# The last group of an FFT convolution in halves, its output sums split into 96 rows first and 32 rows side by side after

## The chip, the cores and the metric

The kernel runs on one core of a Trainium2 chip. The metric is the device time of one execution in microseconds (us), as the median of several runs. TensorE (PE) multiplies matrices into PSUM, VectorE (DVE) and ScalarE (ACT) compute and copy PSUM results into SBUF, GpSimd (POOL) computes tables, SyncE (SP) issues nearly all DMA transfers, and ACT issues a few. A DMA queue issues in order: a transfer that waits for a semaphore holds up all transfers behind it on the same issuing engine.

## The reference

Two state-space convolutions (A and B) run over the same input `u` (2048 steps, 512 channels), and a gate mixes them:

```python
K = jnp.einsum("dn,dnl,dn->dl", Cc, P, dB).real          # a filter for each channel, 2048 long
Yf = Uf * Kf                                             # FFTs over 4096 points
y = irfft2(Yf)[..., :L] + u * Dskip
g = _sigmoid((x * gate_w).sum(-1, keepdims=True))
return g * a + (1 - g) * b
```

All is float32. The output is 2048 x 512 numbers.

## The kernel before, in words

The 512 channels are worked on in eight chunks `c` of 64; a chunk has 128 columns (64 channels of A and of B). For each chunk sixteen-channel steps build the filter from sine and exponential tables (`tables`: ACT, POOL and DVE), and TensorE makes it (`kgen`, L595) and transforms it to a first stage (`first`, L612) in a buffer `xa` or `xb`. That fills nearly all of the run.

Then comes the convolution of a chunk. `conv(c, j)` for j = 0 to 7 makes an eighth of the spectrum with four matmuls (`spectrum`, L625; eight instructions in the trace, since a float32 matmul is recorded as two) and multiplies it on DVE with the spectrum of `u` (L701) into a buffer `y`, of which there are three. After every second `j`, `back(c, U)` (U = 0 to 3, a "unit") transforms back: 32 matmuls (`inv`, L721), each of 64 rows by 64 columns, four of which lie side by side in the array, write two PSUM banks; two copies of 128x512 numbers bring them to `z`; two transfers of 256 KB write `z` to a scratch array `zb` in DRAM; and gathers read `zb` back so that each unit fills 32 partitions of a buffer: for the last chunk `xa`, as one 512 KB transfer for units 0, 1 and 2, and as four transfers of 128 KB, one for each output block, for unit 3. All transfers are issued through `dma` (L295), the copies through `copy` (L300 on ACT, L302 on DVE).

With all four units there, `fin(c, k)` for the output blocks k = 0 to 3 sums over all 128 partitions with the weights `gsi` (the gate is in them): 16 matmuls of 128 rows by 64 columns (L757), one copy of 128x256, and one 128 KB transfer to the output. `stay_awake` (L770) puts six matmuls of 128x512 on TensorE between the sums of chunk 6, and uses their result for nothing.

Nothing is planned at run time: `ORDER` is a list, written out by hand, of all operations by number (a `b` behind a number takes the second engine allowed). Each engine works through its own operations in that order. Buffers are rings: `z` has two, `y` three, the PSUM ring `c` four banks, `s` and `sq` one tile of two banks each. In the end of the list before, TensorE's order is: the inverse of unit 0; spectra 5 and 4; inverse of unit 1; spectra 7 and 6; inverse of unit 2; sums of chunk 6, block 0; inverse of unit 3; sums of blocks 1 and 3 of chunk 6; the six matmuls of `stay_awake`; block 2 of chunk 6; blocks 3, 2, 1 and 0 of chunk 7. SP's order there is: writes of unit 1; gather of unit 0; writes of unit 2; gather of unit 1; writes of unit 3; gather of unit 2; the four gathers of unit 3 with one output transfer among them; the last output transfers.

Of the kernel before, what the change touches and what calls it, by code (L numbers as in the profile page):

```python
# [21 lines left out]
F1, F2 = 32, 64  # L22
# [90 lines left out]
795 796 772 797 1526 1527 1538 798 773 799 1539 785 1553 786b 800 801 787 1554 1540 1541b 1550 1549 1542b 1551 802 803b 886  # L113
# [4 lines left out]
873 1904b 863 864 852 874 875 876 853b 1585 1586 1587 888 892 889 865 893 877 894 895 906 296 896 866 925 878 867 926 897 879  # L118
# [3 lines left out]
1597 1546 1577 1590 1908 1592 1560 1576 1575 1593 1591 331 1612 1915 947 937 948 334 1905 313 314 315b 1916b 316 1917 1578  # L122
1598 1599 323 324b 326 327b 325 960 961 1613 317 949 1614 962 963 318b 1912 320 1918 1020 969 970 988 971 972 987 1023 989 950
951 1913b 964 965 1919b 973 1909 1609 1914 321 322 319 974 975 328 1627 976 920 922 921 977 1910b 978 979 966 967b 990 968 993
# [83 lines left out]
def ssm_mix(ctx: ExitStack, tc: tile.TileContext, a, out, dry=False):  # L208
    slots, pools, shapes = {}, {}, {}

    def ring(tag, n, shape, dtype=F32, space=None):
        slots[tag] = n
        shapes[tag] = shape, dtype
        pools[tag] = space

    ring("xa", 1, [128, F1, CH])
    ring("xb", 1, [128, F1, CH])
    ring("uin", 2, [128, 8, L2])
    ring("par", 2, [128, 5, CH], I32)
# [590 lines left out]
    for c in range(NCH):  # L810
        for k in range(4):
            fin(c, k)
# [45 lines left out]
```

## Time and profile before

| | us |
|---|---|
| median of 3 runs | 432.73 |
| lowest, highest | 431.26, 434.06 |
| the profiled execution, its own time | 429.2 |
| its span (first to last instruction) | 427.4 |
| mean granted TensorE clock in it | 0.994 |

Over the whole span the engines are busy: PE 90%, DVE 90%, ACT 85%, POOL 84%. POOL has done its last work before the last tenth of the span, and the last slices of the profile are of another kind than the rest: there DVE, ACT and POOL are mostly idle, while PE and the DMA engines are not. In the chain of waits, "DMA zb<-z" is a write of `z` to the scratch array, "xa<-zb" a gather for the last chunk, "c<-xa,gsi" the sums of the last chunk and "c<-f,gsi" those of chunks before. Some pieces of the chain are put down to a neighbour: a semaphore is known only by the transfer that the profile links to it.

### The profile page before, as it was taken

How to read it: one execution, taken by the hardware profiler on the slowest of the kernel's cores; microseconds unless marked ns; L12 is line 12 of the kernel's file. 1: busy time of each engine (PE TensorE's matmuls, PEld its weight loads, DVE VectorE, ACT ScalarE, POOL GpSimd, SP SyncE). 2: the span in 40 equal slices, each digit the busy share in tenths (PEclk: the TensorE clock that was granted, in tenths of full speed). 3: DMA queues.
4: the chain of work that ended last, by engine and by line, in shares of the span. 5: the costliest groups of instructions: out<-in, count | busy, mean ns of one | idle time of the engine just before them, and what ended most of it. 6: DMA issues, size and time to landing. Idle time of an engine off the chain costs nothing.

```text
span 427.4 us, 21919 instructions
## 1 busy us (share of the span) xinstructions
PE 384.0 (90%) x9636; PEld 342.3 (80%) x9636; DVE 385.1 (90%) x547; ACT 361.3 (85%) x522; POOL 358.7 (84%) x291
## 2 busy tenths in 40 slices
PE   5898887899998989998989999999889979999994
PEld 5787776788877878888979988888778969898964
DVE  5799999999999999998989999999999999996620
ACT  2889999899998999998889989999899898992211
POOL 1896989899999999997999999999999999970000
PEclk9999999899999999999999999999999999999999
DMA  7968845178882677687385555574777576667794
GB/s 240 287 214 269 263 149 180 28 221 224 257 247 79 197 215 203 201 240 230 109 221 177 176 170 156 166 220 145 225 209 217 143 220 199 172 205 216 219 274 137
DMA packets 79855, 84.63 MB, mean 198 GB/s; under 512 B 7600, under 2 KB 62768, under 8 KB 79664
## 3 DMA queue, kind: packets, MB, share of 16 engines
q1 hardware_dynamic: 79472, 82.96, 65.9%
q8 instruction: 76, 1.25, 1.3%
q10 hardware_dynamic: 288, 0.26, 0.2%
q14 instruction: 19, 0.16, 0.1%
HBM read 51.55 MB, written 31.65 MB: 195 GB/s over the span
## 4 chain that ended last, share of the span: by engine, by line
PE 32%; ACT 23%; DVE 15%; POOL 11%; issue 10%; DMA 7%; SPq 1%; ACTq 0%; DVEq 0%; POOLq 0%
PE c L625 8%; PE c L612 8%; PE c L721 6%; PE c L595 5%; POOL ang L277 4%; DVE mr L287 4%; ACT s L290 4%; POOL mr L277 4%; ACT sq L290 4%; ACT ang L290 3%; PE c L757 3%; DVE ei L277 3%; ACT z L300 2%; DMA zb<-z 2%; DVE y L701 2%
## 5 line engine op out<-in xcount | busy, mean ns | idle before, releaser
L287 DVE SCALAR_TENSOR_TENSOR mr<-sq,mr 128x1024 f32<-128x1024 f32 (+1 forms) x128 | 117.5, 946 | 3.1 <-ACT sq L290 3.0
L277 POOL TENSOR_TENSOR mr<-ml 128x1024 f32<-128x1024 f32 x52 | 101.6, 1955 | 2.5 <-PE c L595 2.0
L277 DVE TENSOR_TENSOR ei<-s,mr 128x1024 f32<-128x1024 f32 x64 | 77.6, 1213 | 2.6 <-POOL mr L277 1.0
L595 PE MATMUL c<-mr 128*32 128x64 f32 x2048 | 64.5, 223 | 8.0 <-DVE mr L287 3.0
L290 ACT ACTIVATE s<-ang 128x1024 f32<-128x1024 int32 x64 | 66.2, 1035 | 6.0 <-DVE ei L287 3.4
L277 POOL TENSOR_TENSOR ang<-sa 128x512 int32<-128x512 int32 x64 | 69.8, 1092 | 0.3
L277 POOL TENSOR_TENSOR ang<-par,cint 128x512 int32<-128x512 int32 x64 | 67.2, 1052 | 3.1 <-ACT sq L290 3.1
L701 DVE TENSOR_TENSOR y<-c,u 128x1024 f32<-128x1024 f32 x57 | 68.7, 1214 | 1.1 <-PE c L625 0.8
L290 ACT ACTIVATE ang<-ang 128x1024 f32<-128x1024 int32 x64 | 67.9, 1061 | 0.9
L290 ACT ACTIVATE sq<-ang 128x1024 f32<-128x1024 f32 x64 | 66.1, 1033 | 2.9 <-DVE mr L287 1.5
L277 POOL TENSOR_TENSOR mr<-mh 128x512 f32<-128x512 f32 x64 | 68.3, 1071 | 0.0
L595 PE MATMUL c<-ei 128*32 128x64 f32 x2048 | 63.6, 221 | 1.4 <-issue 1.4
L612 PE MATMUL c<-small,kt 128*64 128x128 f32 x1024 | 63.0, 275 | 1.6 <-ACT z L300 0.9
L595 PEld LDWEIGHTS c<-mr 128*32 128x32 f32 x2048 | 48.4, 110 | 19.0 <-issue 10.0
L721 PE MATMUL c<-y,vv 64*64 64x128 f32 x1792 | 57.9, 273 | 3.9 <-issue 2.6
L612 PEld LDWEIGHTS c<-small,kt 128*64 128x64 f32 x1024 | 55.5, 137 | 5.4 <-ACT z L300 1.3
L625 PE MATMUL c<-xa,w 128*128 128x128 f32 x384 | 53.0, 284 | 4.6 <-ACT z L300 2.3
L721 PEld LDWEIGHTS c<-y,vv 64*64 64x64 f32 x1792 | 50.1, 133 | 8.4 <-issue 3.7
L625 PE MATMUL c<-xb,w 128*128 128x128 f32 x384 | 51.9, 283 | 5.3 <-DVE c L420 1.6
L625 PEld LDWEIGHTS c<-xb,w 128*128 128x128 f32 x384 | 45.7, 191 | 10.7 <-issue 2.4
L625 PEld LDWEIGHTS c<-xa,w 128*128 128x128 f32 x384 | 45.9, 191 | 9.4 <-ACT z L300 2.9
L595 PEld LDWEIGHTS c<-ei 128*32 128x32 f32 x2048 | 50.4, 111 | 1.6 <-issue 1.5
(108 smaller groups left out, 594.5 us busy)
## 6 DMA issues: line engine op xcount, KB each, us to landing
zb<-z SPq DMA_DIRECT2D x64, 256.0 KB, 3.6
u<-us SPq DMA_DIRECT2D x57, 256.0 KB, 4.1
f<-zb SPq DMA_DIRECT2D x112, 128.0 KB, 3.9
us<-z SPq DMA_DIRECT2D x32, 256.0 KB, 3.1
uin<-in_uk_dram SPq DMA_DIRECT2D x16, 256.0 KB, 4.1
f<-in_ut_dram SPq DMA_DIRECT2D x8, 512.0 KB, 5.6
out_dram<-o SPq DMA_DIRECT2D x28, 128.0 KB, 3.2
par<-prd SPq DMA_DIRECT2D x7, 320.0 KB, 4.2
```

The costliest lines, as they stand in the source:

```text
L277: lambda e: (dve if e == "dve" else pool).tensor_tensor(out=out(), in0=in0(), in1=in1(), op=o),
L287: lambda _: dve.scalar_tensor_tensor(out=out(), in0=in0(), scalar=s, in1=in1(), op0=o0, op1=o1), reads, writes, port=port)
L290: op("act", "act", n, lambda _: act.activation(out=out(), in_=in_(), func=func, **{k: v() if callable(v) else v for k, v in kw.items()}), ...
L300: act.activation(out=o(), in_=i(), func=AF.Copy)
L595: pe.matmul(ps[32 * j:32 * j + 32, o], x[:, 4 * o + j, 64:96], x[:, 4 * o + j, 0:64], start=part == 0, stop=part == 1, tile_position=(0, 3 ...
L612: pe.matmul(t(*ps[g // 4])[64 * r:64 * r + 64, 128 * (g % 4):128 * (g % 4) + 128], t(*x)[:, g], t("small")[:, 128 * r:128 * r + 128], star ...
L625: pe.matmul(view()[:, :, k], t("w2", j // 2)[:, 4 * (j % 2) + k], t(*x1)[:, 4 * j + k], start=True, stop=True)
L701: op("dve", "tt1", 1024, lambda _: dve.tensor_tensor(out=t(*y).rearrange("p h s f d -> p h s (f d)"), in0=fv().rearrange("p s f d -> p s ( ...
L721: pe.matmul(bank_of(x)[64 * e:64 * e + 64, CH * q:CH * q + CH], v[:, 0:64] if h else v[:, 32:96], t(*ys[f // 4])[64 * x:64 * x + 64, h, :, ...
L757: pe.matmul(t(*ps)[64 * r:64 * r + 64, DC * i:DC * i + DC], t("gsi")[:, 4 * k + i, s, 64 * r:64 * r + 64], t(*f)[:, 8 * k + 2 * i + r, DC ...
```

## The change

It touches the last chunk, its order, and two small buffers.

- **The gathers of units 0, 1 and 2 of the last chunk** stay one 512 KB transfer each, but `xa` is now laid out as four eighth-pieces of 8x128 numbers with one spare number behind each (`eighths`), so that a row of 16 KB no longer lies in one piece. `cube` gives the old view of `xa` to all others.
- **Unit 3 of the last chunk in halves** (`w` = 0, 1). A half of the inverse (16 matmuls) needs only one of the two products `y`. It writes halves of two banks of the ring `c`; each half has two copies of 128x256 and two writes of 128 KB.
- **Unit 3's rows over four groups of 32 partitions.** Its four gathers put block k's rows on partitions 32k to 32k+31 of a buffer of the ring `ei` (`spread`), all at the same columns. Four further transfers of 128 KB (`g3`) copy unit 3's weights, rows 96 to 127 of `gsi`, likewise into a buffer of the ring `mr`.
- **The last sums in two steps** (`last_fins`). First, for each block, two matmuls with zero weights clear 256 columns of a PSUM bank, and 16 matmuls sum over the 96 rows of units 0 to 2 (`first_units`). Then the 32 rows of unit 3 are added, two blocks at a time: 32 matmuls of 32 rows by 64 columns whose row groups differ by block (`last_unit`). Blocks 2 and 3 come first. `stay_awake` is gone.
- **The order.** All that lies before the last 250 or so operations stays (it is only renumbered). At the end, TensorE has: inverse of unit 0; spectrum 4; inverse of unit 1; spectra 5 and 7; inverse of unit 2; spectrum 6; sums of chunk 6, block 3; first half of unit 3; block 0; second half; blocks 2 and 1; the first sums of blocks 0, 1, 2, 3; the last sums of 2 and 3; the last sums of 0 and 1. DVE makes products 2, 4, 5, 6, 7 in this order, then copies one piece of the first half. ACT copies the other piece of the first half and both of the second. SP has: writes of unit 1; gather of unit 0; writes of unit 2; gather of unit 1; gather of unit 2; the first half's two writes; an output transfer, `g3` of block 2, another output transfer, `g3` of block 3; the gathers of unit 3 for blocks 2 and 3; output transfers. ACT's queue has the second half's two writes, the gathers of unit 3 for blocks 0 and 1, and output transfers. `g3` of blocks 0 and 1 stand on SP much earlier, among the gathers of chunk 6.
- **`dummy`**, one column used to load a table of ACT at the start, becomes a fifth column of `gate_w`. The gathers of chunks 0 to 6 get an access pattern written with one dimension less; what they move is the same.

The core of the diff (the order's numbers left out):

```diff
-    ring("xa", 1, [128, F1, CH])
+    ring("xa", 1, [128, 4 * (8 * CH + 1)])
...
         last = c == NCH - 1
         ys = [("y", c, 2 * U + i) for i in range(2)]
-        ps = [(("s", "sq")[U % 2], "inv", U)] if last else [("c", "inv", c, U, x) for x in range(2)]
+        wide = last and U < 3
+        parts = 2 if last and not wide else 1
...
+        for w in range(parts):
+            ps = [(("s", "sq")[U % 2], "inv", U)] if wide else [("c", "inv", c, U, x, w) if last else ("c", "inv", c, U, x) for x in range(2)]
+            qs = slice(4 // parts * w, 4 // parts * (w + 1))
...
+            op("pe", "inv", 128 // parts, inv, [*(ys if parts == 1 else ys[w:w + 1]), ("vv", U // 2)], ps, table="square")
+            for x in range(2):
+                copy(512 // parts, lambda x=x, qs=qs: t(*z)[:, x, qs].rearrange("p q k -> p (q k)"),
...
+                if parts > 1:
+                    g = 8 * U + 4 * x
+                    dma(128, lambda g=g, x=x, qs=qs: t(*zb)[g + qs.start:g + qs.stop].rearrange("g p k -> p g k"),
+                        lambda x=x, qs=qs: t(*z)[:, x, qs], [zx], [("zu", c, U, x, w)], True, touch=[z, zb])
+        if parts > 1:
+            for k in range(4):
+                dma(128, lambda k=k: spread()[32 * k:32 * k + 32],
+                    lambda k=k: t(*zb)[8 * U:8 * U + 8].rearrange("g (m a) k -> (g m) a k", m=4)[:, 8 * k:8 * k + 8],
...
+        if last:
+            dma(512, lambda: eighths(f)[32 * U:32 * U + 32, :, 0:8 * CH],
+                lambda: t(*zb)[8 * U:8 * U + 8].rearrange("g (m h a) k -> (g m) h (a k)", m=4, h=4),
...
-    def stay_awake():
...
+    def spread():
+        return t("ei", "fin").rearrange("p a b -> p (a b)")[:, 0:8 * CH].rearrange("p (a k) -> p a k", k=CH)
+
+    def last_fins():
+        c, K = NCH - 1, 96
+        f, g3 = home(c), ("mr", "gsi")
+        gv = lambda: t(*g3).rearrange("p a b -> p (a b)")[:, 0:1024].rearrange("p (i s m) -> p i s m", i=4, s=2)
+        for k in range(4):
+            dma(128, lambda k=k: gv()[32 * k:32 * k + 32], lambda k=k: t("gsi")[K:128, 4 * k:4 * k + 4],
...
+        def first_units(_, k):
+            for r in range(2):
+                pe.matmul(acc(k)[64 * r:64 * r + 64], t("small")[0:K, 3:256:4], t("small")[0:K, 0:256],
+                          start=True, stop=False, tile_position=(0, 64 * r))
+            for i in range(4):
+                for s in range(2):
+                    for r in range(2):
+                        pe.matmul(acc(k)[64 * r:64 * r + 64, DC * i:DC * i + DC], t("gsi")[0:K, 4 * k + i, s, 64 * r:64 * r + 64],
+                                  eighths(f)[0:K, k, CH * (2 * i + r) + DC * s:CH * (2 * i + r) + DC * s + DC], start=False, stop=False, tile_position=(0, 64 * r))
+
+        def last_unit(_, ks):
+            for i in range(4):
+                for s in range(2):
+                    for r in range(2):
+                        for k in ks:
+                            rows = slice(32 * k, 32 * k + 32)
+                            pe.matmul(acc(k)[64 * r:64 * r + 64, DC * i:DC * i + DC], gv()[rows, i, s, 64 * r:64 * r + 64],
+                                      spread()[rows, 2 * i + r, DC * s:DC * s + DC], start=False, stop=i == 3 and s == 1, tile_position=(32 * k, 64 * r))
...
-    stay_awake()
+    last_fins()
```

More of the change, by code (lines that the diff above doesn't have):

```diff
@@ L236, in ssm_mix @@
         "logdt": [128, NCH],
-        "dummy": [128, 1], "small": [128, 525], "gsi": [128, 16, 2, 128], "gate_w": [128, 4],
+        "small": [128, 525], "gsi": [128, 16, 2, 128], "gate_w": [128, 5],
         "dt": [128, 3, NCH], "ex": [128, NCH], "ek": [128, NCH], "er": [128, NCH], "ea": [128, NCH]}
@@ L267, in t @@
     def t(*key):
+        if key in (("dummy",), ("gate_w",)):
+            return tiles["gate_w",][:, 4:5] if key == ("dummy",) else tiles["gate_w",][:, 0:4]
         if key not in tiles:
@@ L731, in back @@
+        if parts > 1:
+            for k in range(4):
+                dma(128, lambda k=k: spread()[32 * k:32 * k + 32],
+                    lambda k=k: t(*zb)[8 * U:8 * U + 8].rearrange("g (m a) k -> (g m) a k", m=4)[:, 8 * k:8 * k + 8],
+                    [("zu", c, U, x, w) for x in range(2) for w in range(2)], [("ei", "fin")] * (k == 0) + [("fs", k)], True,
+                    touch=[zb] + [("ei", "fin")] * (k > 0))
+            return
         for x in range(2):
@@ L734, in back, with eighths, cube @@
                 [("zx", c, U, x)], [zb] * (new and x == 0) + [("zu", c, U, x)], touch=[z] + [zb] * (not (new and x == 0)))
[L735 to L741 removed]
+        if last:
+            dma(512, lambda: eighths(f)[32 * U:32 * U + 32, :, 0:8 * CH],
+                lambda: t(*zb)[8 * U:8 * U + 8].rearrange("g (m h a) k -> (g m) h (a k)", m=4, h=4),
+                [("zu", c, U, 0), ("zu", c, U, 1)], [f] * new + [("fu", c, U)], touch=[zb] + [f] * (not new))
+            return
+        for h in range(4):
+            dma(128, lambda h=h: t(*f)[32 * U:32 * U + 32, 8 * h:8 * h + 8].rearrange("p a k -> p (a k)"),
+                lambda h=h: t(*zb)[8 * U:8 * U + 8].rearrange("g (m a) k -> (g m) a k", m=4)[:, 8 * h:8 * h + 8].rearrange("p a k -> p (a k)"),
+                [("zu", c, U, 0), ("zu", c, U, 1)], [f] * (new and h == 0) + [("fu", c, U, h)],
                 touch=[zb] + [f] * (not (new and h == 0)))
+    def eighths(f):
+        return t(*f).rearrange("p (h x) -> p h x", h=4)
+    def cube(x):
+        return t(*x)[:, 0:F1 * CH].rearrange("p (f k) -> p f k", k=CH) if x[0] == "xa" else t(*x)
     def home(c):
@@ L760, in fin @@
         op("pe", "fin", 64, mm, [("gsi", n) for n in ((0, 1), (2, 3))[k % 2]] + [("fu", c, U, k) for U in range(4)], [ps], table="fin", touch=[f])
-        copy(256, ov, lambda: t(*ps)[:, 0:256].rearrange("p (i d) -> p i d", i=4), [ps], [o])
-        dma(128, lambda: out[:, c, 4 * k:4 * k + 4], ov, [o], (), c >= NCH - 2)
-    def stay_awake():
-        ps = ("c", "awake")
-        def mm(_):
-            for _ in range(6):
-                pe.matmul(t(*ps), t("w2", 0)[:, 0], t("w2", 1)[:, 0:4].rearrange("p f m -> p (f m)"), start=True, stop=True)
-        op("pe", "warm", 24, mm, [("w2", 0), ("w2", 1), ("sq", "inv", 3)], [ps], table="full")
+        copy(256, lambda: t(*o), lambda: t(*ps)[:, 0:256].rearrange("p (i d) -> p i d", i=4), [ps], [o])
@@ L809, in ssm_mix @@
                 back(c, j // 2)
-    for c in range(NCH):
+    for c in range(NCH - 1):
         for k in range(4):
             fin(c, k)
-    stay_awake()
+    last_fins()
     if dry:
```

87 lines of the change are left out of this document (48 added, 39 removed), and 42 rows, old and new, of the table ORDER.

## The prediction

> **What bounds the kernel now.** All engines are near full until the last tenth, and the change leaves the order before that alone, so I read the page only for the span and then the end: first the chain of waits in order of time.
>
> ```profile
> span 427.4 us, 21919 instructions
> ...
> 396.74 1.91 PE s L721 x64
> 398.65 1.98 PE c L625 x16
> 400.63 1.91 PE sq L721 x64
> 402.54 1.98 PE c L625 x16
> 404.52 1.91 PE s L721 x64
> 406.43 1.08 PE c L757 x32
> 407.51 1.95 PE sq L721 x64
> ...
> 409.53 0.60 ACT z L300
> ...
> 410.16 0.70 DVE z L302
> ...
> 410.88 5.03 DMA zb<-z
> ...
> 416.85 2.74 DMA out_dram<-o
> 419.59 0.06 issue
> 419.65 3.96 PE c L757 x128
> ...
> 423.69 0.38 ACT o L300
> ```
>
> Columns: start, length, what. Unit 3's inverse starts at 407.51, its second copy ends at 410.86, the write to DRAM takes 5.03 us, and the last sums (64 matmuls, 128 records) run from 419.65 to 423.61. The piece put down to an output transfer is really the first gather of unit 3. Then SP's own timeline, with times from issue to landing (smallest, median, largest) for unit 0's two writes, unit 2's two writes, unit 0's gather, unit 2's gather, and unit 3's four small gathers, in this order.
>
> ```profile
> 403.27 1.80 SPq L295 DMA_DIRECT2D zb<-z  x2
> 405.25 0.37 SPq L295 DMA_DIRECT2D xa<-zb  x1
> 407.16 0.91 SPq L295 DMA_DIRECT2D zb<-z  x2
> 408.17 0.45 SPq L295 DMA_DIRECT2D xa<-zb  x1
> 410.15 1.11 SPq L295 DMA_DIRECT2D zb<-z  x2
> 412.97 3.79 SPq L295 DMA_DIRECT2D xa<-zb  x3
> ```
>
> ```profile
> DMA to landing us min/median/max: 2.5/2.8/3.1
> DMA to landing us min/median/max: 5.0/5.1/5.2
> DMA to landing us min/median/max: 5.3/5.3/5.3
> DMA to landing us min/median/max: 5.8/5.8/5.8
> DMA to landing us min/median/max: 3.3/3.3/3.4
> ```
>
> ```profile
> 403.00:404.00 1.00, 1.00 (x11) 1.00 (x10) 1.00 (x2) 0.74 (x2) 0.00 (x0) 1.00 0.21 45
> 404.00:408.00 4.00, 4.00 (x121) 3.64 (x123) 2.18 (x2) 1.09 (x2) 0.00 (x0) 1.00 0.90 242
> 408.00:412.00 4.00, 4.00 (x118) 3.52 (x111) 1.22 (x3) 0.60 (x1) 0.00 (x0) 1.00 1.06 276
> 412.00:416.00 4.00, 4.00 (x11) 1.79 (x10) 0.23 (x1) 0.00 (x0) 0.00 (x0) 1.00 1.08 298
> ```
>
> The last two columns are the DMA engines' share and GB/s. A write alone lands in 2.5 to 3.1 us; from 404 to 416 the DMA engines are full and the same write takes 5. So the end is a chain of transfers behind a full set of DMA engines, and TensorE only fills time: unit 2's gather, issued at 412.97, lands at 412.97 + 5.8 = 418.8, unit 3's first gather at 415.97 + 3.4 = 419.4. Both reach the sums almost together, and only then 3.96 us of sums begin.
>
> **The change, part by part.** The profiled execution's own time is 429.2 us, 1.8 more than its span; the median of the runs, 432.73, is 3.5 above that. I work out the change of the span and add it to the median.
>
> *Unit 3 in halves.* Needed besides the chain are the products on DVE, and the groups.
>
> ```profile
> 398.71 1.23 DVE L701 TENSOR_TENSOR y<-c,ml 128x1024 f32<-128x1024 f32 x1 [1.13 <-PE s L721]
> 402.60 1.22 DVE L701 TENSOR_TENSOR y<-c,mh 128x1024 f32<-128x1024 f32 x1 [1.53 <-PE sq L721]
> 405.62 1.22 DVE L701 TENSOR_TENSOR y<-c,mh 128x1024 f32<-128x1024 f32 x1 [0.66 <-PE s L721]
> ```
>
> ```profile
> L770 PE MATMUL c<-w,w 128*128 128x512 f32 x12 | 5.4, 601 | 0.0
> L721 PE MATMUL sq<-y,vv 64*64 64x128 f32 x128 | 4.0, 272 | 0.0
> L757 PE MATMUL c<-xa,gsi 128*64 128x64 f32 x128 | 4.0, 223 | 1.8 <-DMA out_dram<-o 1.8
> ```
>
> A product waits for the inverse that frees its buffer. In the new order product 2 still ends at 398.71 + 1.23 = 399.9; the spectrum of 4 (half of 1.98) is done by then, so unit 1's inverse ends at 401.85 (now 402.54). Spectrum 5 to 402.85, product 5 to 404.1, unit 2's inverse to 406.0 (now 406.43), spectrum 6 to 407.0. Products 6 and 7 come one after the other, to 408.2 and 409.4. On TensorE block 3 of chunk 6 (1.08) goes to 408.1, the first half-inverse (0.95) to 409.2; block 0 needs the bank that product 7 reads, 409.4 to 410.5; the second half to 411.45. ACT copies both its pieces (128x256, 0.38 each as in the row of 423.69) by 412.25. Unit 3 is thus complete 1.4 us later than now (410.86): the halves gain nothing, because spectrum 6 has moved behind unit 2's inverse. Blocks 2 and 1, the first waiting for a bank until 411.9, end at about 414.0.
>
> *The queues.* Unit 2's copies end at 407.2 (two of 0.60 after 406.0), its writes are issued at 406.7 and 407.3. Unit 0's gather comes after unit 1's writes, which come 0.7 earlier; the DMA engines stand at 0.21 at 403, so it is issued at about 404.0 and not 405.25, and less is queued ahead of unit 2's writes: landing after between 3.1 us (a write alone) and 5.2 (as now); I take 4.1, nearer to now by the queue, so 411.4. Then SP issues unit 2's gather at 411.5; now it goes out at 412.97, when those writes (the second issued about 407.7, 5.0 to 5.2 to landing) are there. Its landing takes between 3.4 us (a 128 KB gather) and 5.8 (as now). Its pieces of 4 KB in place of 16 KB may help, four small writes join it; I take 5.0, near unit 0's 5.3: **416.5**.
>
> Unit 3's first-half writes stand on SP behind that gather and its wait, and are issued at 411.9 and 412.3; the second half's on ACT at 412.3 and 412.7, where behind them only copies and output transfers of chunk 6 wait, which nobody needs. Landing after 3.1 to 5.2, so 415.8 to 417.9: 417.0. Its four gathers, two on each queue, then issue by 417.5 and land by **420.8 to 421**.
>
> *The last sums.* Clearing: six matmuls of 512 columns took 5.4 us, so 0.45 for 256 columns, and the pair for the two column halves lies side by side as the pairs of L757 do; if it didn't, 0.9. The 16 matmuls of a block are a quarter of 3.96, 0.99: the 32 rows fewer save no time, since the moving columns are the same. So the first sums take 4 x 1.44 = 5.8 us (up to 7.6), from 416.5 to 422.3. The last sums: the inverse does 32 matmuls of 128 columns, four side by side, in 1.91, so 32 of 64 columns take 0.99, if two row groups of 32 run together as those of 64 do; if not, 1.98. Twice: 2.0 (up to 4.0), to 424.3. Unit 3's rows, there at 421, wait for nothing more. Now the sums end at 423.61: **+0.7**.
>
> *The rest.* The end of the span:
>
> ```profile
> 423.12 1.76 SPq L295 DMA_DIRECT2D out_dram<-o  x2
> 425.50:426.00 0.50, 0.00 (x0) 0.00 (x0) 0.00 (x0) 0.00 (x0) 0.00 (x0) 1.00 0.62 207
> 426.00:426.50 0.50, 0.00 (x0) 0.00 (x0) 0.00 (x0) 0.00 (x0) 0.00 (x0) 0.60 0.00 0
> ```
>
> From the last sum to the end are 3.8 us now. The last two outputs go out on two queues and not one: between 0 and 0.4 less, I take 0.1. The four `g3` transfers cost nothing while they land before 421; the two late ones follow unit 3's writes, and without that cover each costs 128 KB at the 276 GB/s above, 0.5 us. `dummy` and the other access patterns touch nothing that is waited for. Sum: +0.7 - 0.1 = +0.6, a span of 428.0 and a time of 432.73 + 0.6 = **433.3 us**. What the change really does is exchange 3.96 us of sums after the last landing for 7.8 after an earlier one.
>
> *What the removed matmuls did.* In the last two rows the column before the share is the granted clock: 1.00 until 426.0, then 0.60 as a mean over half a microsecond, so halved at 426.1, 2.5 us after the last matmul. The 5.4 us of L770 stood where TensorE would otherwise idle. In the new order it idles from 414.0 to 416.5, just that long. I take the clock as held, and the other case as a rival. The Trainium skill, "TensorE: Matmul & The Clock Gate", section "What's actually happening", states that one idle window of about 3.4 us halves the clock and one busy window of that length restores it; by it a 2.5 us gap need not trip the gate, and if it did, the estimate is 1.7 us more. The trace's fall after 2.5 us of idleness is sooner than that figure, and its return no row shows.
>
> **The rivals.**
>
> *Slower: the clock falls in the gap.* For it: the fall 2.5 us after the last matmul, and a gap of 0.4 to 4 us by the bounds above. Against: a gap of 1.8 us before the last sums (the row of L757) cost nothing, and the matmuls after it took 223 ns as ever. Price: nothing shows how long the clock takes to come back; if as long as it took to fall, 2.5 us at half clock lose 1.25 (434.5); at most all 7.8 us double (441.1). It decides for "slower" once more than 3.7 us of the block's work runs at half clock.
>
> *Unit 2's gather lands no sooner than now*, at 418.8, the DMA engines being as full as before and the bytes more by `g3`: +2.3 on my sum, 435.6. For it: the share of 1.06 to 1.08; against: the earlier start of units 0 and 1 that I worked out.
>
> *Unit 3's path sets the end*, unit 2 landing by 415: the sums end at 420.8 + 2.0 = 422.8, time 431.8. This is also the floor: to be over 1% (4.3 us) faster the sums would have to end by 419.3, before unit 3's rows land. Only a shift elsewhere could do that.
>
> *The row groups of 32 don't run together*: +2.0, 435.3.
>
> **How the numbers follow.** Chances: the forecast 0.42; unit 3's path 0.19; the clock 0.17, of it 0.07 with the price above 3.7; unit 2 late 0.12; row groups 0.05; a shift of the whole kernel, since addresses and the order from about 383 on change, 0.05, half each way. What a measurement can tell from no change is 1%, 4.3 us. Faster by more: 0.025 from a shift, and 0.035 for an end that I mis-sized, 0.06. Slower: 0.07 from the clock, 0.025 from a shift, 0.03 for two of the slower cases together, 0.125, say 0.13. The rest, 0.81, is within 1%. The runs of one kernel lie 1.4 us either side of their median; the range goes from 431.8 less that, 430.4, to 435.6 plus that, 437.0.
>
> **What would show it.** In the chain of waits the last sums should follow a block of first sums of about 5.8 us, and that should follow unit 2's gather, landing near 416.5; unit 3's gathers should be there before the first sums end. If the chain goes through unit 3's gathers, the third rival holds. Records of the first sums well above 223 ns and a granted clock under 1.00 around 417 to 420 show the clock. Second-half copies before 411 would prove my order of spectrum 6 and product 7 wrong; a last-sums pair of about 2 us, the row groups. The prediction fails if the last matmul ends before 421 or after 428.

## The result and the profile after

| | before | changed |
|---|---|---|
| median of 4 runs, us | 432.18 | 437.62 |
| lowest, highest | 431.26, 434.06 | 436.31, 439.32 |
| ratio, 95% interval | | 1.0121 (1.0079 to 1.0164) |
| the profiled execution, its own time | 429.2 | 437.17 |
| its span | 427.4 | 434.4 |
| around the span | 1.8 | 2.8 |
| records of matmuls | 9636 | 9768 |

The change makes the kernel 1.2% slower, about 5 us, where 0.6 us were forecast; the time lies above the range. "Around the span" is the part of an execution's own time that lies outside its first and last instruction; a float32 matmul is two records in the profile. The ratios here and below leave disturbed executions out, so they need not equal the quotient of the medians.

The chain of waits of the changed kernel, in order of time (start, length, what), from the end of the transform of the parameters on:

```profile
394.65 1.12 issue
...
401.88 1.95 PE s L730 x64
...
416.79 0.41 ACT z L303 x2
417.20 5.43 DMA zb<-z
422.64 0.02 issue
422.66 0.54 SPq L298
...
423.24 0.58 SPq L298
...
423.86 0.54 SPq L298
...
424.51 0.51 SPq L298
425.02 0.04 issue
425.07 3.32 DMA ei<-zb
...
428.43 0.98 PE sq L820 x52
...
430.06 0.17 issue
430.24 0.63 PE s L820 x25
```

Before, this chain went from the write of `zb` through a gather of unit 3 to 3.96 us of sums. Now the sums behind the gather are short (428.43 to 430.87, 2.44 us), but between the write's landing at 422.64 and the gather's issue at 425.07 stand 2.4 us in which SP only issues. SP's timeline shows what:

```profile
413.05 4.37 SPq L298 DMA_DIRECT2D xa<-zb  x2
417.47 1.96 SPq L298 DMA_DIRECT2D zb<-z  x2
419.48 0.49 SPq L298 DMA_DIRECT2D out_dram<-o  x1
422.66 0.54 SPq L298 DMA_DIRECT2D mr<-gsi  x1
423.24 0.58 SPq L298 DMA_DIRECT2D out_dram<-o  x1
423.86 0.54 SPq L298 DMA_DIRECT2D mr<-gsi  x1
424.51 0.98 SPq L298 DMA_DIRECT2D ei<-zb  x2
```

After the output of 419.48 SP waits until 422.66 with the `g3` copy of block 2 (`mr<-gsi`), then issues it, an output, the second `g3`, and only then unit 3's gathers, half a microsecond each. That copy needs no row of unit 3. But in the built program every transfer signals one of eight semaphores in turn, and is held until the transfer eight places ahead of it has landed; eight places ahead of this one is a write of unit 3 (in the trace that write signals semaphore 103, and the copy waits on 103). ACT's timeline has the other two gathers:

```profile
424.08 0.38 ACT L303 ACTIVATE o<-c 128x256 f32<-128x256 f32 x1 [6.63 <-DMA out_dram<-o]
424.23 0.94 ACTq L298 DMA_DIRECT2D ei<-zb  x2
```

They stand behind a copy of chunk 6 that waits for an output to land.

TensorE meanwhile (same kernel, TensorE's timeline; in brackets the idle time ahead and what ended it):

```profile
420.12 0.39 PE L783 MATMUL c<-f,gsi 128*64 128x64 f32 x6 [0.99 <-issue]
...
422.42 1.15 PE L811 MATMUL s<-xa,gsi 96*64 96x64 f32 x32 [1.35 <-DMA zb<-z]
...
426.74 1.10 PE L811 MATMUL sq<-xa,gsi 96*64 96x64 f32 x32
...
428.43 0.98 PE L820 MATMUL sq<-ei,mr 32*64 32x64 f32 x52 [0.34 <-DMA ei<-zb]
```

Unit 2's rows are there at 422.42, the four first sums take until 427.84 (1.42 us from one block to the next, 1.44 in the forecast), and the last gather lands at 428.4. "issue" is a wait that nothing in the program explains; what these are, the later runs show. Of the loads of instructions, the page counts this for the span (packets, MB, share):

```profile
q8 instruction: 76, 1.25, 1.2%
```

and a look at the stretch from 434 to 438 us, which begins just ahead of the last instruction, shows one more, where the stretch behind the end of the kernel before (427.4 to 433 us) has no packet at all:

```profile
DMA packets 1, 0.02 MB, mean 4 GB/s; under 512 B 0, under 2 KB 0, under 8 KB 0
## 3 DMA queue, kind: packets, MB, share of 16 engines
q8 instruction: 1, 0.02, 1.4%
```

Where the 5 us went, by the two profiles: from the start of unit 0's inverse to the last matmul 26.9 us before, 29.0 now (+2.1); from there to the end of the span 3.8 and 3.5 (-0.3); around the span, over all executions, 1.8 and 2.5 (+0.7). The rest, 2 to 3 us, lies ahead of unit 0's inverse (396.7 and 401.8), but there the two profiled executions compare badly: that of before is 3.0 us faster than its median, that of the changed kernel 0.5.

### The profile page after: what moved, and what is told of

The parts are those of the page before. It is cut to its first block, busy times and chain, and to the rows that moved or that the text cites. A ratio compares the mean times of both kernels' runs of the same rounds, so it can differ in the third digit from the quotient of the medians.

```text
span 434.4 us, 22192 instructions
## 1 busy us (share of the span) xinstructions
PE 384.9 (89%) x9768; PEld 344.2 (79%) x9768; DVE 387.2 (89%) x550; ACT 360.8 (83%) x521; POOL 359.0 (83%) x291
## 4 chain that ended last, share of the span: by engine, by line
PE 31%; ACT 27%; DVE 19%; issue 11%; DMA 6%; POOL 4%; SPq 1%; ACTq 0%; DVEq 0%; POOLq 0%
PE c L628 8%; PE c L615 7%; PE c L730 6%; DVE mr L290 6%; PE c L598 6%; ACT s L293 5%; ACT ang L293 4%; ACT sq L293 4%; DVE ei L280 4%; DVE y L704 3%; ACT z L303 3%; PE c L783 2%; DMA uin<-in_uk_dram 2%; ACT xa L303 2%; ACT mh L534 1%
## 5 line engine op out<-in xcount | busy, mean ns | idle before, releaser
L730 PE MATMUL c<-y,vv 64*64 64x128 f32 x1856 | 60.4, 273 | 5.6 <-issue 4.1
L598 PEld LDWEIGHTS c<-mr 128*32 128x32 f32 x2048 | 48.3, 109 | 19.3 <-issue 12.0
L730 PEld LDWEIGHTS c<-y,vv 64*64 64x64 f32 x1856 | 52.0, 133 | 10.5 <-issue 5.5
L303 ACT ACTIVATE z<-c 128x512 f32<-128x512 f32 (+1 forms) x76 | 42.8, 589 | 18.7 <-PE c L730 16.2
```

Of the source, the lines that this page charges most:

```text
L303: act.activation(out=o(), in_=i(), func=AF.Copy)
L598: pe.matmul(ps[32 * j:32 * j + 32, o], x[:, 4 * o + j, 64:96], x[:, 4 * o + j, 0:64], start=part == 0, stop=part == 1, tile_position=(0, 3 ...
L730: pe.matmul(bank_of(x)[64 * e:64 * e + 64, CH * q:CH * q + CH], v[:, 0:64] if h else v[:, 32:96], t(*ys[f // 4])[64 * x:64 * x + 64, h, :, ...
```

## The experiments

The first four runs ask where the loss lies: theory **E** in their expectations says in the end alone, theory **B** there says in the whole run, by something in the change such as the layout. The later runs test four theories, and B has another meaning in them. **A**: TensorE's clock falls to half in the end, since the idle matmuls are gone. **B**, later **C**: the way of the rows through DRAM and the queues sets the end; lateness of unit 3's gathers (B), or the landings of both units, behind which the split sums put more work than before (C). **D**, formed on the traces of the first runs: the change has 132 more records of matmuls, and loading instructions costs time. Idle matmuls feed nothing. "Around" is the mean time around the span, "clock" the mean granted clock, as a share of TensorE's full clock.

| run | median | ratio to before | 95% | clock | around | records |
|---|---|---|---|---|---|---|
| before (five groups) | 431.9 to 434.3 | | | 0.994 | 1.8 | 9636 |
| after_again | 437.61 | 1.0109 | 1.0063 to 1.0155 | 0.988 | 2.5 | 9768 |
| layout_only | 432.07 | 1.0000 | 0.9972 to 1.0029 | 0.994 | 1.8 | 9636 |
| after_old_layout | 436.75 | 1.0126 | 1.0081 to 1.0170 | 0.989 | 2.3 | 9768 |
| gathers_first | 437.52 | 1.0134 | 1.0089 to 1.0179 | 0.987 | 2.4 | 9768 |
| before_no_warm | 433.39 | 1.0004 | 0.9970 to 1.0039 | 0.985 | 1.8 | 9624 |
| after_warm | 436.95 | 1.0082 | 1.0044 to 1.0119 | 0.992 | 2.4 | 9772 |
| unit3_early | 438.36 | 1.0108 | 1.0054 to 1.0163 | 0.987 | 2.7 | 9768 |
| all_four | 436.87 | 1.0086 | 1.0052 to 1.0121 | 0.992 | 2.6 | 9772 |
| sums_only | 436.71 | 1.0114 | 1.0074 to 1.0155 | 0.992 | 1.9 | 9780 |
| halves_only | 434.71 | 1.0063 | 1.0034 to 1.0091 | 0.991 | 1.8 | 9630 |
| outs_sp | 435.79 | 1.0073 | 1.0033 to 1.0113 | 0.987 | 2.4 | 9768 |
| early_sums_and_unit3 | 436.44 | 1.0081 | 1.0043 to 1.0118 | 0.989 | 2.6 | 9768 |
| more_instructions | 436.37 | 1.0104 | 1.0066 to 1.0141 | 0.993 | 1.9 | 9912 |
| sums_cleared | 435.31 | 1.0063 | 1.0019 to 1.0107 | 0.995 | 1.9 | 9780 |
| outputs_late | 432.04 | 0.9999 | 0.9961 to 1.0038 | 0.993 | 1.8 | 9636 |
| same_count | 434.73 | 1.0075 | 1.0036 to 1.0114 | 0.992 | 2.6 | 9768 |

### The layout, and the place of the gathers

**after_again**: the changed kernel once more, beside the next three.

> The changed kernel once more, as the control for the three others. In the two profiles 5.2 of the 7.0 us that separate the spans lie ahead of unit 0's inverse in the last chunk, where the order of the work is the same but for the last 12 us; only 1.9 lie behind it. Theory E (the end): only the end is slower, the rest is the luck of two single executions: the difference of the medians shrinks to 2 to 3 us (ratio 1.005 to 1.007), and in the new profile unit 0's inverse starts within 1.5 us of 396.7. Theory B (the body): something in the change slows all of the run: ratio 1.010 to 1.015 again, and unit 0's inverse starts at 400 to 403.

**layout_only**: the kernel before with the new buffers alone.

```diff
-    ring("xa", 1, [128, F1, CH])
+    ring("xa", 1, [128, 4 * (8 * CH + 1)])
```

> The kernel before with the new layout of xa, the gathers of units 0 to 2 in pieces of 4 KB, and dummy inside gate_w; its order, unit 3 and the last sums as before. Theory B by the layout (addresses, pieces): 2 to 4 us slower than before. Theory E: body as before; the pieces of 4 KB let unit 2's gather land at most 1 us sooner than the 5.8 us of before, and as unit 3's path is as long, the time is the same within 1 us.

**after_old_layout**: the changed kernel with `xa` as before; the same two lines the other way round.

> The changed kernel with xa laid out as before (rows of 16 KB in one piece, dummy on its own). Theory B by the layout: 2 to 4 us faster than the changed kernel. Theory E: as the changed kernel within 1 us; unit 2's gather lands 5.8 us after its issue and not 5.0 to 5.6, but the end is set by unit 3's gathers, which have slack to neither side.

**gathers_first**: the changed kernel with another order at the end. 1869 is unit 2's gather, 1886 to 1889 unit 3's, 1976 and 1977 the late `g3` copies, 1970 and 1973 outputs, 1963 ACT's copy.

```diff
-1857 1869 1882 1885b 1883b 1878 1880 1970 1976 1973 1977 1963 1886b 1966b 1888 1889
+1857 1976 1977 1869 1882 1885b 1883b 1878 1880 1970 1886b 1887b 1888 1889 1973 1963 1966b
```

> The changed kernel with unit 3's four gathers at the head of both queues: g3 of blocks 2 and 3 is issued ahead of unit 2's gather, and the copy and the outputs of chunk 6 that stood before the gathers come behind them. In the profile of the changed kernel SP's gathers went out 1.85 and 2.4 us after unit 3's writes had landed (422.64), and ACT's 1.6 and 2.0 us, behind g3, an output and a copy that waited for an output buffer. Theory E with the queue as the bound: the gathers land at about 426.5 on that clock and the first sums (to 427.8) set the end: 0.8 to 1.2 us faster than the changed kernel. Rival: the first sums and unit 2's gather set the end anyway: no change within 0.4 us.

The loss repeats: 1.0109 is what B had forecast, but in the profile unit 0's inverse starts at 399.24, later than E had said and sooner than B. The layout has no part in it: new buffers alone 1.0000, the changed kernel without them 1.0126. Nor did the queues' order help: 437.52, where 0.8 to 1.2 us less than the changed kernel was forecast. In the profile of gathers_first the gathers are no longer waited for; the first sums ran at half clock instead. The windows view (stretch, its length, busy us of TensorE and its records, weight loads, DVE, ACT, POOL, granted clock, DMA share, GB/s), cut where the clock changes:

```profile
418.51:421.92 3.41, 0.94 (x11) 0.55 (x11) 0.00 (x0) 0.00 (x0) 0.00 (x0) 1.00 0.75 181
421.92:425.34 3.42, 3.38 (x52) 3.01 (x54) 0.00 (x0) 0.17 (x1) 0.00 (x0) 0.50 0.30 89
425.34:428.75 3.41, 3.41 (x58) 3.04 (x57) 0.09 (x1) 0.21 (x1) 0.00 (x0) 0.50 0.74 221
428.75:432.16 3.41, 3.41 (x170) 3.26 (x168) 0.76 (x2) 0.15 (x1) 0.00 (x0) 1.00 0.14 43
```

and the kernel before, cut the same way:

```profile
415.86:419.27 3.41, 2.00 (x35) 1.10 (x33) 0.42 (x1) 0.00 (x0) 0.00 (x0) 1.00 0.64 172
419.27:422.69 3.42, 3.04 (x104) 3.07 (x106) 0.00 (x0) 1.15 (x3) 0.00 (x0) 1.00 0.36 119
422.69:426.10 3.41, 0.92 (x32) 0.78 (x27) 0.00 (x0) 0.77 (x2) 0.00 (x0) 1.00 0.48 156
426.10:427.40 1.30, 0.00 (x0) 0.00 (x0) 0.00 (x0) 0.00 (x0) 0.00 (x0) 0.50 0.00 0
```

In every profile the clock changes only at steps of one grid of 3.41 us (in the kernel before it falls at 77.94 and at 426.1, 102 steps apart). Counted over all 18 profiles, a stretch at full clock with TensorE busy for 1.4 us or less was always followed by half clock, one with 1.6 to 1.8 us sometimes, one with 2.0 to 2.25 in only four cases, among them the changed kernel's own last sums (2.25 us, of 32 rows). By these counts a gap of 2 us costs nothing or 3.4 us at half clock, by where it lies on the grid, which is another place in each execution. The Trainium skill, "TensorE: Matmul & The Clock Gate", section "What's actually happening", has the window (3413 ns, free-running), and the trace agrees (102 steps in 348.16 us); it lets the clock fall after an idle window, where here 0.94 us of work in it did not prevent that.

### The clock by itself

**before_no_warm**: the kernel before without its six idle matmuls.

```diff
-    stay_awake()
```

> The kernel before without the six matmuls of its helper `stay_awake`, everything else as it was. Theory A (TensorE's clock is granted anew for each stretch of 3.41 us, and halves after a stretch in which TensorE was busy for less than about 40%; these matmuls were there to prevent that): TensorE is idle for some 7 us before the last sums, so the clock is half for 3.4 to 6.8 us there, and the last sums (3.96 us at full clock) lose 2 to 4 us: 434 to 436 us, mean granted clock near 0.986. Rival (the clock comes back at once, or the last sums do not depend on it): 431 to 433 us, as before.

**after_warm**: the changed kernel, two idle matmuls of 128x512 behind chunk 6's last block.

```diff
+            for _ in range(2):
+                pe.matmul(t(*ps), t("w2", 0)[:, 0], t("w2", 1)[:, 0:4].rearrange("p f m -> p (f m)"), start=True, stop=True)
```

> The changed kernel with two matmuls of 128x512 (1.8 us) put in front of the first sums, where TensorE waits for unit 2's gather. Theory A (the clock): the fall before the first sums no longer happens, the one between the first and the last sums may: mean granted clock 0.989 to 0.994 and 435 to 436 us, where the changed kernel has 437.6. Rival (the loss lies in unit 3's gathers and in nothing that TensorE's clock does): 437 to 438 us.

Without the idle matmuls the clock does fall in the kernel before: mean 0.985 in place of 0.994, and in its profile (TensorE's timeline) the last sums last 5.69 us, not 3.96:

```profile
423.90 5.69 PE L766 MATMUL c<-xa,gsi 128*64 128x64 f32 x128 [6.91 <-DMA out_dram<-o]
```

Yet its time stays at 1.0004; the interval leaves room for the 1.7 us at its very end, not for 2 to 4. With the clock restored in the changed kernel (0.992), 436.95 remain, where A had 435 to 436. So theory A describes the clock rightly, but no run shows a part of the loss to come from it: the ratios differ by some 1.5 us, within their intervals.

### Unit 3 early, and everything together

**unit3_early**: in the order, spectrum 6 (1871) ahead of unit 2's inverse (1864) and 7 behind, both half-inverses (1876, 1881) ahead of chunk 6's blocks, and so on as the expectation tells.

```diff
-1874 1864 1865 1871 1866 1872 1875 1971 1876 1962 1877 1879b 1881 1884 1968
+1871 1864 1865 1874 1866 1872 1875 1876 1877 1879b 1881 1884 1971 1962 1968
-1857 1869 1882 1885b 1883b 1878 1880 1970 1976 1973 1977 1963 1886b 1966b 1888 1889
+1857 1878 1880 1869 1882 1885b 1883b 1970 1886b 1887b 1888 1889 1973 1963 1966b
```

> The changed kernel with unit 3 made early: spectrum 6 ahead of unit 2's inverse and 7 behind it, the two halves of unit 3's inverse ahead of chunk 6's blocks, their first writes ahead of unit 2's gather on SyncE, all four g3 copies at the end of the transform of the parameters, and unit 3's gathers ahead of the outputs of chunk 6. Its rows should land near 22.5 us after unit 0's inverse begins and not 26.6, so before the first sums end; the last sums then follow without a wait, 0.6 us earlier. Theory B (unit 3's gathers set the end): 436.5 to 437 us, and no wait for ei<-zb in front of the last sums. Theory A (the clock) beside it: TensorE idles for over 4 us before the first sums, so that the clock is half in them in nearly every execution, mean granted clock 0.985: 437 to 440 us, no better than the changed kernel.

**all_four**: besides, the clearings in operations of their own, ahead of the first sums and behind two idle matmuls.

```diff
-        def first_units(_, k):
+        def clear(_, k):
             for r in range(2):
                 pe.matmul(acc(k)[64 * r:64 * r + 64], t("small")[0:K, 3:256:4], t("small")[0:K, 0:256],
                           start=True, stop=False, tile_position=(0, 64 * r))
+
+        def first_units(_, k):
```

> The kernel with unit 3 made early, and besides the four clearings of the sums ahead of the first sums and not between them (they need no rows), and two matmuls of 128x512 ahead of those, so that 3.6 us of TensorE's wait for unit 2's gather are filled. Theories A and B together: first sums 3.9 us and not 5.4 after unit 2's gather, last sums 2.0 to 2.4 behind them without a wait, clock full: last matmul 26.5 to 27 us after unit 0's inverse begins (changed kernel 29.0, before 26.9), mean granted clock 0.992 to 0.995, 432.5 to 434 us. If only the clock counts: 435. If neither: 437.

Unit 3's rows came early enough: in neither profile does a gather hold the last sums. But no time was won. In unit3_early the first sums run at half clock, as theory A had warned (0.50 from 421.95 to 428.77), a block taking 1.98 us and not 1.15:

```profile
422.22 1.98 PE L819 MATMUL s<-xa,gsi 96*64 96x64 f32 x32 [2.37 <-DMA xa<-zb]
```

Nor do its rows come as early as its transform: unit 3's writes go out 11.9 to 13.6 us after unit 0's inverse begins (13.5 to 14.2 before), and still its gathers cannot be issued before 19.1 (before 19.3): the four half-size writes take, by the list of transfers (count, size, median us to landing),

```profile
zb<-z SPq DMA_DIRECT2D x2, 128.0 KB, 5.6
zb<-z ACTq DMA_DIRECT2D x2, 128.0 KB, 5.4
```

as long as the 256 KB write of before, 5.03, and from 412.8 to 420 the DMA engines' share is 1.09: what is started sooner waits longer while they are full. all_four is the cleaner test of theory B in its narrow form, since its clock holds there, and it goes against it: 436.87 where 432.5 to 434 were forecast. Its TensorE timeline shows what replaced the waits:

```profile
420.57 0.45 PE L791 MATMUL c<-f,gsi 128*64 128x64 f32 x8 [1.62 <-issue]
...
431.14 0.68 PE L830 MATMUL s<-ei,mr 32*64 32x64 f32 x29 [1.04 <-issue]
```

Two waits for nothing that the program names, one of them in the middle of the last sums: 2.66 us together, about what separates the last matmul, 29.2 us after unit 0's inverse begins, from the forecast of 26.5 to 27. I counted such waits in the 18 profiles of this study: 193 waits of TensorE on "issue" above 0.2 us. Of these 187 stand at only 26 places of the instruction stream, which recur from kernel to kernel (record 4407 in all 18, 7201 in 16, 9489 in 11) and lie, from record 1740 to 9743, at multiples of one step, 127 records. They last 0.2 to 2.3 us, and each of the 187 ends 1.1 to 1.7 us after a load of 16 KB on the instruction queue. TensorE's instructions are loaded in blocks; where a block is late, TensorE stands. It is late mostly where TensorE works its records off fast: of the blocks of 127 records that took TensorE under 4.5 us, 143 of 380 were followed by such a wait, of those that took over 5.5 us, 3 of 515. The Trainium skill, "Runtime: NRT & Kernel Launch", section "Instruction fetch mechanics", states blocks of 16 KiB or 256 instructions, which agrees (127 matmuls and their weight loads are 254), and calls the crossing mostly hidden; here 7 to 15 of some 76 crossings in an execution are not, 5 to 16 us together.

### One part of the change alone

**sums_only**: order, transform and idle matmuls of before, the sums and the layout of the change (`g3` early). The line shown is against the changed kernel, and so is that of halves_only.

```diff
-        wide = last and U < 3
+        wide = last
```

> One part alone: the order and the undivided transform of the kernel before, its six idle matmuls too, but the sums of the last chunk split as in the change (first sums over 96 rows, then the last 32 rows side by side; the g3 copies early). Theory C (the way of the rows through DRAM sets both landings, a write of about 5 us and then a gather of about 6 us, and the split sums put 7.8 us of work behind unit 2's landing where 3.96 us stood behind unit 3's): unit 2 lands about 22.2 us after unit 0's inverse begins, the last matmul is at 30 us (before 26.9): 435 to 436.5 us. Rival (the split sums cost nothing, the loss comes from unit 3's halves and their place in the queues): 432 to 433 us, as before.

**halves_only**: unit 3 in halves and early, gathered into the last 32 partitions for sums over 128 rows, as before, with three idle matmuls.

```diff
-                dma(128, lambda k=k: spread()[32 * k:32 * k + 32],
+                dma(128, lambda k=k: eighths(f)[32 * U:32 * U + 32, k, 0:8 * CH],
```

> The other part alone: unit 3 in halves and as early as in the run with unit 3 made early, its rows gathered into the last 32 partitions, and the sums of the last chunk undivided over 128 rows as before (3.96 us), with three idle matmuls in front of them. Theory C: unit 3's rows land 22.5 to 23.5 us after unit 0's inverse begins (before 23.0) although its transform is done sooner, and the last matmul is at 26.5 to 27.5 us: 432 to 433.5 us, no gain and no loss. Rival (halves and their queues cost the time): 435 us and more.

**outs_sp**: the changed kernel, the last outputs issued by SyncE (a "b" in the order gives a transfer to ScalarE).

```diff
-1985b 1990 1991b 1983 1989 1986b 1984
+1989 1985b 1990 1991 1983 1986 1984
```

> The changed kernel with all four of the last chunk's outputs issued by SyncE, as before, and not two of them by ScalarE. If the time around the span (2.7 us in the changed kernel, 1.8 before) hangs on ScalarE's transfers, it goes back to 1.8 and the time to 436.6 us or a little above, since SyncE issues them one after the other; if not, 437.5 us.

**early_sums_and_unit3**: all_four without idle matmuls, and with the outputs of outs_sp.

> The changed kernel with all that its losses ask for: unit 3 early (as in that run), the four clearings ahead of the first sums so that these take 3.9 us and not 5.4, no idle matmuls, all last outputs on SyncE. Theory C: unit 2 lands 20.6 to 21.3 us after unit 0's inverse begins, first sums to 25.2, last sums to 27.3 (28.3 if TensorE waits for instructions in them): 433 to 434.5 us, still no better than before. Rival (only lateness inside the changed kernel held it back): 26 us and 431 to 432 us, better than before.

The split sums alone lose nearly all that the change loses, 1.0114. Their profile (TensorE's timeline; unit 0's inverse begins at 401.06) has what theory C gives:

```profile
423.42 1.15 PE L826 MATMUL s<-xa,gsi 96*64 96x64 f32 x32 [0.67 <-DMA xa<-zb]
...
427.70 1.13 PE L826 MATMUL sq<-xa,gsi 96*64 96x64 f32 x32
428.76 0.99 PE L835 MATMUL sq<-ei,mr 32*64 32x64 f32 x52
```

Unit 2 lands 22.4 us after that start, and 7.5 us of sums follow: last matmul at 29.9 (forecast 30, before 26.9). That is 3 of its 4.9 us, and between unit 0's inverse and the last matmul this profile has no wait on "issue" above 0.2 us: late blocks are no part of these 3. halves_only was forecast at 432 to 433.5 and has 434.71: the halves are no gain, and 1.5 to 3.9 us of loss by the interval. Its profiled execution, the slowest of its twelve, has a late block (2.17 us, at record 9488) and last sums at half clock (6.29 us), though the kernel has six records fewer than before; one execution doesn't show whether these are the usual loss. outs_sp contradicts its theory: the time around the span is 2.4 with SyncE as with ScalarE. early_sums_and_unit3 misses its forecast as all_four did, with late blocks of 1.20 and 1.82 us in its sums.

### The instructions

**more_instructions**: the kernel before, its idle matmuls many and small.

```diff
-            for _ in range(6):
-                pe.matmul(t(*ps), t("w2", 0)[:, 0], t("w2", 1)[:, 0:4].rearrange("p f m -> p (f m)"), start=True, stop=True)
+            for _ in range(72):
+                for r in range(2):
+                    pe.matmul(t(*ps)[64 * r:64 * r + 64, 0:64], t("w2", 0)[:, 0][:, 0:64], t("w2", 1)[:, 0][:, 0:64], start=True, stop=True,
+                              tile_position=(0, 64 * r))
```

> The kernel before, its six idle matmuls of 512 columns (12 records) replaced by 144 of 64 columns, side by side in pairs, about as long together: TensorE gets as many matmuls as in the changed kernel, 9768, and computes the same. Theory D (TensorE's instructions are loaded in blocks of 16 KB, one for about 127 matmuls, and the change brings one block more): 77 loads and not 76; where the last comes behind the span's end the time around the span is 2.5 us and not 1.8, and the time is 0.5 to 1.5 us above before. Rival (instructions cost only their own time): no change, within 0.5 us of before.

I had counted a matmul as one record; it is two. So the records of idle matmuls are twice as many as meant, they last 11.3 us, and delay the last sums themselves; on the question the 1.0104 says nothing. Its timeline shows the blocks well, though, in a run of equal matmuls that wait for nothing else:

```profile
413.67 0.86 PE L771 MATMUL c<-w,w 128*64 128x64 f32 x23
415.09 3.95 PE L771 MATMUL c<-w,w 128*64 128x64 f32 x128 [0.55 <-issue]
420.48 4.47 PE L771 MATMUL c<-w,w 128*64 128x64 f32 x137 [1.44 <-issue]
```

**same_count**: the same with half as many, 9768 records in all like the changed kernel.

```diff
-            for _ in range(72):
+            for _ in range(36):
```

> The kernel before, its six idle matmuls (12 records in the profile, 5.4 us) replaced by 72 of 64 columns, side by side in pairs (144 records, 4.5 us at the 31 ns that one took in the run with more of them): 9768 records of matmuls as in the changed kernel, and the sums of before. Theory D (132 more records are one more block of instructions, and that costs time beyond their own): 77 loads; TensorE waits 0.5 to 1.5 us for a block among the idle matmuls, which their place hides; where the 77th load comes behind the span's end, 2.5 us around the span and not 1.8; so 0.5 to 1 us above before. Rival (a block of instructions costs nothing that the end shows): within 0.3 us of before.

The sums, the transform, the order of the queues and the layout are those of before, the clock is 0.992, and the kernel is 0.75% slower (0.36 to 1.14), 3.2 us, more than theory D had said. 0.8 us of it lies around the span (2.6 and 1.8), and the profile shows how a late block gets from an idle place to the end. TensorE's timeline, then the chain:

```profile
418.82 0.40 PE L757 MATMUL c<-f,gsi 128*64 128x64 f32 x7
420.94 0.97 PE L757 MATMUL c<-f,gsi 128*64 128x64 f32 x25 [1.72 <-issue]
...
427.37 1.54 PE L757 MATMUL c<-xa,gsi 128*64 128x64 f32 x32 [2.66 <-DMA xa<-zb]
```

```profile
419.22 1.72 issue
420.94 0.98 PE c L757 x25
...
421.95 0.44 DVE o L302
...
422.41 2.58 DMA out_dram<-o
...
425.00 2.24 DMA xa<-zb
```

The block boundary falls into a block of sums of chunk 6 that nobody is in a hurry for. Its copy is late, so its output is late, and SP holds the last gather of unit 3 until that output has landed (the eight semaphores again); the last quarter of the sums waits 2.7 us for it.

Two more things differ from before here, so that the 3.2 us are not the price of 132 records alone. In the trace of before the last gather shares its semaphore, 106, with a write of unit 3, and this output has 107; here the output has 106, so the gather must wait for it. before_no_warm has the same pairing, without records added, and its time is that of before (1.0004): the pairing alone shows no cost. And the six long idle matmuls have become short ones: TensorE works off the two blocks around them in under 4 us each, where a block is often late, and in before it took 9.1 us over the first of them. The run shows what 132 more records can cost in a dense stretch, not what they cost anywhere.

The time around the span goes with the last block. Of the ten profiles of kernels with 9768 or 9772 records, six have 2.46 to 2.92 us around the span, and in all six the 77th load comes 1.8 to 2.1 us after the last instruction, as in the changed kernel above; three have 1.7 or 1.8 us, and there it was done before the end; one has 2.1 us and no 77th load on record. With 9780 records it comes 1.0 us after the end, at 1.9 to 2.1 us around.

**sums_cleared**: sums_only with the clearings ahead of the idle matmuls, in operations of their own as in all_four.

> The kernel with the split sums alone (the order and the transform of before), the four clearings moved ahead of the idle matmuls, so that after unit 2's landing the first sums take 3.9 us and not 5.4. If the sums behind that landing set the end, as theory C says, it gains all of it, 1.4 us on the run with the split sums alone: last matmul 28.5 us after unit 0's inverse begins, and about 435 us. Rival (that run's loss lies in front of unit 0's inverse, by where instructions or data lie): no gain, 436 to 437 us.

435.31, as forecast, 1.4 us below sums_only, though the two intervals overlap. That the gain lies where it was said to lie is not shown: in the profile the sums behind unit 2's landing take 6.1 us in place of 7.5, but the rows land 23.5 us after unit 0's inverse begins and not 22.4, and the last matmul is at 29.6, not 28.5.

**outputs_late**: the kernel before, chunk 6's outputs (1959, 1962, 1965, 1968) behind unit 3's gathers (1881 to 1884). This kernel lists the blocks of chunk 7 in another order, so its numbers 1969 to 1974 are 1975 to 1980 of before, and the other way round.

```diff
-1968b 1958b 1964b 1879 1880 1869 1884 1978 1883 1959 1975 1882 1965b 1972 1881 1961 1962 1969 1979
+1958b 1964b 1879 1880 1869 1884 1972 1883 1969 1882 1978 1881 1959 1962 1975 1973 1968b 1974 1970 1965b
```

> The kernel before with the four outputs of chunk 6 issued behind unit 3's gathers (two of the copies go to other buffers, so that nothing waits for that), and these four gathers in one go. Theory C (writes and gathers through DRAM, slowed by what else the DMA engines move, set the end): units 2 and 3 land 0.5 to 1.2 us sooner and the sums end by 26.4 us after unit 0's inverse begins, not 26.9: 431 to 432 us where before has 432.3, the version that would beat both. Rival (the outputs lie beside them and take nothing, or the end then waits for them): 432 to 433 us.

0.9999 (0.9961 to 1.0038). In its profile the last matmul is 26.3 us after unit 0's inverse begins, as forecast, but the time doesn't show it: a gain of the size hoped for is not excluded, and none is shown. No version beat the kernel before.

## Why the prediction was wrong

**TensorE up to the two halves: right.** Counted from unit 0's inverse (5.14 us later than before), unit 2's inverse ends at 405.9 (said 406.0), product 7 at 409.35 (409.4), the second half's copies at 412.3 (412.25). That unit 3 is complete 1.4 us later than before was right too.

**Unit 2's gather: nearly.** Issued at 411.7 and landed at 417.3 on that scale, where 411.5 and 416.5 were said: 0.8 us late, but 1.5 us sooner than before, so the rival "no sooner than now" falls.

**"Its four gathers, two on each queue, then issue by 417.5": wrong**, the step on the chain that failed. They were issued at 419.1 to 419.9 and landed at 423.2, not 421. I had let `g3` and the outputs cost their issue at most, and written of ACT that behind the writes only copies and outputs wait "which nobody needs"; but the gathers stood behind those copies and outputs. Of the +2.1 us at the last matmul in place of +0.7, this step is 0.6, the wait between first and last sums; 0.8 is the landing of unit 2. It is not the whole of the loss: where the gathers came in time (gathers_first, unit3_early, all_four), the time stayed, with half clock or late blocks in their place.

**The sums: right.** First sums 5.42 us (said 5.8), last sums 2.44 (2.0), row groups side by side: together they are off by under 0.1 us. And so was the remark that the change exchanges 3.96 us of sums for 7.8 behind an earlier landing: sums_only has the 7.5 without the earlier landing and loses 3 us at that place.

**"I take the clock as held": half right.** It held in the profiled execution until the last sums were done, fell in others (mean 0.988), and no run shows what that is worth: after_warm has a ratio of 1.0082 where the changed kernel has 1.0109 to 1.0121, about 1.5 us that the intervals don't separate. That "nothing shows how long the clock takes to come back" was an oversight: in the trace of before it is at half from 77.94 to 81.35, one step of 3.41 us.

**The term that was missing** is the loading of instructions. The sum had prices for matmuls by their durations, and none for 132 more records, one block of 16 KB; the time around the span was taken as unchanged, and what lies outside the end as "a shift of the whole kernel", 0.05 and half each way. The runs show 2.5 us around the span with the 77th load behind the end, +0.7, and late blocks of up to 2.2 us in the end of kernels with the changed order. The profile of before did not hide the waits: 10% of its chain that ended last is put down to "issue". In the changed kernel's own profile the late block in the end (0.99 us at 420.12) lies ahead of a wait for unit 2's gather, and isn't in the chain shown; so what the +2.1 us have over the forecast is the two steps above, and the 3.2 us of same_count can't be put in their place.

The sum as measured is +2.1 at the last matmul, -0.3 behind it, +0.7 around the span, and 2 to 3 us ahead of unit 0's inverse. That the split sums cost 3 us when unit 2 lands no sooner is shown (sums_only); that the count of records makes up the rest of the loss is not, since every kernel with the split sums has the longer stream as well.

**Open**: how much of the 2 to 3 us ahead of unit 0's inverse is the change's; with it the cause of half of the loss stays open. 1.12 us of it is one wait for instructions at 394.65, at a place where before has none. Seven of the nine profiles with the changed order have such a wait there or one block earlier (0.2 to 1.1 us), and one of the nine others (0.2 us). The rest is within what executions of one kernel differ by, and no run here separates it. Why halves_only loses is open as well.

## What to carry to other kernels

Count the instructions of a change, not only their durations: in this kernel of thousands of small matmuls each 127 more records are a block to load, and a late block stops TensorE for up to 2 us. That was common where a block was worked off in under 4.5 us, so look at how dense the matmuls are as well as how many, and at what stands at the next boundary. Before forecasting when a transfer is issued, read in the built program which semaphore it shares with a transfer that has not landed; a copy that needs nothing can hold the whole queue, and a change elsewhere can deal the semaphores anew. And where DMA engines are full, a transfer that is split and issued earlier need not land earlier.

## What was not expected of the hardware

- TensorE waits for its own instructions: 26 places, multiples of 127 records apart, 0.2 to 2.3 us, 7 to 15 times an execution, and differently in each; after 143 of 380 blocks that it worked off in under 4.5 us, and after 3 of 515 that took over 5.5.
- In the six profiles whose last block is loaded some 2 us behind the last instruction, the program ends later by its own time: 2.5 to 2.9 us around the span and not 1.8.
- The granted clock changes on a grid of 3.41 us only, and in these profiles up to 1.4 us of work in a stretch were never enough to hold it.
- Pieces of 16 KB in a gather and pieces of 4 KB make no difference in the time (1.0000, interval 0.9972 to 1.0029).
